# Pooled attention and a top-1 mixture of experts: gate stores, a query load and routing work moved to other places in the schedule

## The chip, the cores and the metric

The kernel runs on one core of a Trainium2 chip. The metric is the device time of one execution, in microseconds (us). A core has a matrix engine (TensorE, PE in the profile, with its weight loads as PEld), VectorE (DVE), ScalarE (ACT), GpSimd (POOL) and SyncE (SP), which issues most of the DMA transfers here. Each engine works off its own instructions in the order in which the program emits them, and engines wait for one another by semaphores. Schedules here are written by hand: moving a call in the source moves its instructions in the queues.

## The reference

```python
def _attn_ref(q, k, v):                      # 8 batches, 8 heads, 576 rows, 64 columns
    k_p = k.reshape(B, H, Sp, pool, D).mean(axis=3)      # pool = 8, Sp = 72
    v_p = v.reshape(B, H, Sp, pool, D).mean(axis=3)
    scores = scale * np.matmul(q, k_p.transpose(0, 1, 3, 2))
    attn = np.exp(scores - np.max(scores, axis=-1, keepdims=True))
    attn = attn / (np.sum(attn, axis=-1, keepdims=True) + 1e-09)
    return np.matmul(attn, v_p)

def _moe_ref(x, modality_id, w_gate, modality_bias, w1, w2):   # 4608 tokens, 512, 8 experts, 1024
    logits = x @ w_gate + modality_bias[modality_id]
    e_idx = np.argmax(logits, axis=1)
    probs = softmax(logits)
    gate_w = probs[np.arange(N), e_idx]
    for e in range(E):
        h = np.maximum(x[mask] @ w1[e], 0.0)
        out[mask] = gate_w[mask, None] * (h @ w2[e])
```

The attention's output, with the heads side by side in a row of 512, is the `x` of the second function. All is in 32-bit floats; the expert matmuls split each operand into a high and a low part and use three products.

## The kernel before, in words

**Attention.** Eight batches are worked off as 20 steps (`steps`, N = 20): of each pair of batches two steps of the first (two token tiles of 128 each), a mixed step with one tile of both batches' last 64 rows, and two steps of the second. Four pairs give four groups of nine tiles (`GROUPS`). The main loop (`for n in range(N + 1)`) emits in each step: the loads of that step (`loads(n)`), transposes of probabilities (`t_pe`, L692), scores (`s_pe`, L657 for a mixed tile, L663 for others), their maximum and difference on VectorE (`s_dve`, L670 and L673), exp on ScalarE (`s_act`), the weighted sum of values (`a_pe`, L727 and L731), its division on VectorE (`x_dve`, L750 to L760) and the query transposes of the next steps (`q_pe`, L638). The weighted sum has one PSUM buffer, the score tiles and the shared transpose tiles (tag `tr`) two each. Keys and values are summed over groups of eight rows, most of that on GpSimd (`fold`, L417 to L419), two batches ahead for keys and one for values.

**Hooks.** Work that belongs to no step is hung at places in the step: `hook_0` at its start, `hook_1` before the first weighted sum, `hook_q` after the query transposes, `hook_2` before the second weighted sum, `hook_3` at the end (of step N - 1 it is run early in step N).

**Loads.** `step_loads` lists which loads SyncE issues in which step, in that order; after them come the stores of token rows (`xs<-xb`, L767 and L770) that the step before made ready. `xs` is a table in DRAM with a row for each token: 512 values of the attention's output, then columns for the gate and for factors.

**Routing.** `route(g)` returns a list of small VectorE operations for a group: sums of the logits (L809), bias, maximum, difference and exp (`sub`, L816, L817), the choice of the expert (L820 to L822), the softmax's sum, `gates` (L844: the gate values; then four stores of 4-byte elements into the gate column of `xs`, L847 and L849), the running counts (L852), the rank matmuls `pe` (L829 to L833), ranks (L858 to L867) and nine rows `arow` (L869). They are put into `drip` and emitted one or two at a time at each `gap()`, between other VectorE work. `pe` is held: it is emitted only by `release()` in the step after one near whose end it stood first in the list. Groups 0 to 2 start two steps after their last step; the last group's list (`last_route`) is emitted after the loop and in the first expert slots. After group 1 the list also finds the first slots' tokens (`early_table`) and gathers them from `xs`.

**Start of the experts.** During the last attention steps the first expert's weights are loaded into `raw`, split into a high part on ScalarE (`split0`, L966) and a low part on VectorE (`split_lo`, L141), the first slot's tokens are transposed (`x_transposes`, L174 to L177), and the first layer of that slot is computed in eight blocks (`first0`, L184 on PE, L186 on ScalarE, L188 `h` on VectorE, by `finish()`), each with a PSUM tile of the tag `tr`. Then come the expert slots of 256 tokens (`part(s)`), in which PE runs two layers for each slot. Slot 0 has only the second layer left (`slot0`, L1365); `late` lists what small work is emitted after which of its eight blocks, such as `counts` (L1171), the rest of the last group's routing and the tables for later slots. For slot 1 the tokens are rearranged through DRAM (`blocks_out`, L246 for the copy of the gate column, L261, L266; `blocks_in`, L280).

Of the kernel before, what the change touches and what calls it, by code (L numbers as in the profile page):

```python
# [24 lines left out]
EARLY_GROUPS = 2  # L25
# [8 lines left out]
def kernel(  # L34
# [12 lines left out]
    nc = tc.nc  # L47
# [92 lines left out]
    def split_lo(f, eng):  # L140
        eng.tensor_sub(hl[f][:, 1, :], raw[f], hl[f][:, 0, :].bitcast(F32))  # L141
# [103 lines left out]
    def keep_gate(s, tt, eng):  # L245
        eng.tensor_copy(gc[:, 2 * s + tt:2 * s + tt + 1], xg[(2 * s + tt) % 4][:, D:D + 1])  # L246
# [4 lines left out]
    def blocks_out(s, tt):  # L251

        x = xg[(2 * s + tt) % 4] if tt < 2 else xe
        to = xg[(2 * s + 2 + tt % 2) % 4][:, 0:D]
        xp = to.rearrange("p (j k r) -> p j k r", j=NQ, r=QUAD)
        f = x[:, RX:RX + H].rearrange("p (k a o q) -> p k a o q", a=2, o=1, q=1)
        for a in range(2):
            xo = xp[:, 2 * a:2 * a + 2].rearrange("p j k r -> p k j r")
            xi = x[:, 0:D].rearrange("p (k a j r) -> p a k j r", k=ND, a=2, j=2)[:, a]
            if s < EARLY_SLOTS:  # L260
                nc.scalar.copy(xo, xi)  # L261
            else:
                nc.vector.tensor_tensor(xo, xi, f[:, :, a].to_broadcast([P, ND, 2, QUAD]), op=ALU.mult)
        if tt < 2:
            keep_gate(s, tt, nc.vector)
        nc.sync.dma_start(scr[s % 2, tt * P:(tt + 1) * P, :], to)  # L266

    def blocks_in(s, tt):
# [29 lines left out]
    with ExitStack() as actx:  # L298
# [302 lines left out]
        for g, (t0, n) in enumerate(GROUPS):  # L601
            for t in range(t0, t0 + n):
                tile_group[t] = (g, t - t0)
        drip, held, stores = [], set(), []

        def gap(n=2):

            for _ in range(n):
                if drip and drip[0] not in held:
                    drip.pop(0)()  # L610
# [180 lines left out]
        def route(g):  # L791
# [50 lines left out]

            def gates():
                V.reciprocal(gate[:, sl], sm)  # L844
                for z in range(2):
                    b = 2 * g + z
                    nc.sync.dma_start(xs[b * S:b * S + 512, D:D + 1].rearrange("(p j) o -> p (j o)", j=4),  # L847
                                      gate[:, t0 + 5 * z:t0 + 5 * z + 4], allow_slow_non_contiguous=True)
                    nc.sync.dma_start(xs[b * S + 512:(b + 1) * S, D:D + 1],  # L849
                                      gate[64 * z:64 * z + 64, t0 + 4:t0 + 5], allow_slow_non_contiguous=True)  # L850
            add(gates)
            add(lambda: V.tensor_add(cum[:, g + 1, :], cum[:, g, :], dc))  # L852
            held.add(pe)
# [91 lines left out]
        def at(hook, n, *fns):  # L945
            hook.setdefault(n, []).extend(fns)
# [19 lines left out]
            nc.scalar.copy(hl[f][:, 0, z * D:(z + 1) * D], raw[f][:, z * D:(z + 1) * D])  # L966

        for g in range(len(GROUPS) - 1):
            n = s1_of[2 * g + 1] + 2
            def start(g=g):  # L970
                ops = route(g)
                drip.extend(ops)
                if g == 0:
                    drip.extend(first_expert())
            at(hook_0, n, start)
            if g == EARLY_GROUPS - 1:
                at(hook_0, n, lambda: drip.extend(early_table()))
        for f, n in enumerate((10, 11, 11, 12, 13, 13, 14, 15)):
            at(hook_1, n, lambda f=f: (new_raw(f), load_w(0, f)))
        for f, n in enumerate((12, 13, 14, 15, 15, 16, 17, 19)):  # L980
            at(hook_1, n, lambda f=f: split0(f, 0))
            at(hook_2, n, lambda f=f: split0(f, 1))
        for f, n in enumerate((15, 15, 16, 16, 17, 17, 18, 19)):
            at(hook_3, n, lambda f=f: split_lo(f, nc.vector))
        at(hook_2, N - 3, lambda: x_transposes(0, xg, (0,)))
        at(hook_3, N - 3, lambda: x_transposes(0, xg, (1,)))
        at(hook_1, N - 2, lambda: keep_gate(0, 0, nc.gpsimd), lambda: keep_gate(0, 1, nc.gpsimd),
           lambda: blocks_out(1, 0), lambda: blocks_out(1, 1))
        at(hook_1, N - 1, lambda: blocks_in(1, 0), lambda: blocks_in(1, 1))
        for f in range(NF):  # L990
            at((hook_1, hook_2, hook_3)[(f + 1) % 3], N - 2 + (f + 1) // 3, lambda f=f: first0(f))

        at(hook_0, 5, modality_terms)

# [8 lines left out]


        step_loads = {}
        for n, fn, b in ((0, load_k, 2), (0, load_k4, 2), (0, load_v, 2), (0, load_v4, 2), (0, load_k, 3), (1, load_q, 2),
                         (1, load_v, 3), (1, load_k4, 3), (1, load_routing, None), (1, load_k, 4), (2, load_qmix, 1),
                         (2, load_v4, 3), (2, load_v, 4), (3, load_k4, 4), (4, load_q, 3), (4, load_k, 5), (4, load_v4, 4),
                         (4, load_v, 5), (5, load_k4, 5), (5, load_k, 6), (6, load_q, 4), (6, load_v4, 5), (6, load_v, 6),
                         (7, load_qmix, 2), (7, load_k4, 6), (7, load_k, 7), (9, load_q, 5), (9, load_v4, 6), (9, load_v, 7),  # L1010
                         (10, load_k4, 7), (11, load_q, 6), (11, load_v4, 7), (12, load_qmix, 3), (14, load_q, 7)):
            step_loads.setdefault(n, []).append((fn, b))

        def loads(n):
            for fn, b in step_loads.get(n, ()):
                fn(b) if b is not None else fn()
            while stores:
                stores.pop(0)()

        pool_k(0, (0,))  # L1020
        k_operand(0, 0)
# [25 lines left out]
        for n in range(N + 1):  # L1047
# [43 lines left out]
            run(hook_q, n)  # L1091
            if old:
                x_dve(old[0])
            gap(2)
            if nxt and n:
                q_act(n + 1, 1)
# [168 lines left out]
    for i, r in enumerate(EXTRA):  # L1265
# [14 lines left out]
    late = {  # L1280
        (0, 0): [lr[9], lr[7], lr[11], lr[8]],
        (0, 1): [lr[10]],
        (0, 3): [counts, lr[12]] + [fn for pair in zip(bases, lr[13:20]) for fn in pair] + [lr[20]],
        (0, 4): lr[21:24],
        (0, 5): lr[24:27],
        (0, 6): lr[27:],
        (1, 2): experts,
        (1, 3): columns,
        (1, 4): changes,
# [375 lines left out]
```

## Time and profile before

| what | us |
|---|---|
| median of 3 runs | 590.39 |
| the runs | 586.99, 590.39, 590.56 |
| the profiled execution | 587.84 |
| its span on the core | 586.0 |

Busy time in the span, from the page: PE 565.6 us (97%), PEld 494.6 (84%), DVE 371.3 (63%), ACT 277.6 (47%), POOL 183.5 (31%). By stages: the attention runs from the start to about 180 us, the expert slots from there to the end; the last slot's tail begins near 560.

How to read the rows below. A row of the busy time by stretch has the stretch, its length, then for PE, PEld, DVE, ACT and POOL the busy time with the number of instructions in brackets, then the granted TensorE clock as a share of full speed, the mean busy share of the 16 DMA engines and GB/s. A row in order of time has start, duration, engine, line, operation, what it writes and reads by name, partitions and elements, how many instructions were merged, and in brackets the engine's idle time before it with what ended it. Rows of SPq are issues of DMA transfers by SyncE; their duration is that of issuing, not of the transfer. The chain of waits gives start, duration and what the end of the execution hung on in that time. Matmuls are pipelined and their ends are modelled, so start-to-start distances are safer than durations.

### The profile page before, as it was taken

The numbers are of one execution on the slowest core, as the hardware profiler recorded it, in microseconds if no ns is written. First come the engines' busy times: TensorE is split into PE (matmuls) and PEld (weight loads), VectorE is DVE, ScalarE is ACT, GpSimd is POOL, SyncE is SP. The second block draws the span as 40 slices with busy tenths as digits, with TensorE's granted clock in tenths as the row PEclk, the third lists the DMA queues.
The fourth block names the chain that finished last, engine by engine and source line by source line (L and its number), as shares of the span: only waits on it lengthen the run. The fifth ranks groups of instructions, "written<-read, shape, count | busy, mean of one in ns | idle before, by whom it ended". The sixth has DMA issues, their size and how long they took to land.

```text
span 586.0 us, 11992 instructions
## 1 busy us (share of the span) xinstructions
PE 565.6 (97%) x3487; PEld 494.6 (84%) x3487; DVE 371.3 (63%) x939; ACT 277.6 (47%) x656; POOL 183.5 (31%) x290
## 2 busy tenths in 40 slices
PE   5999999999999999999999999999999999999995
PEld 5789888998898888888888888888888888888994
DVE  6887898778967676466456457856455497465211
ACT  2767676798652434333334336634334474334110
POOL 7679969854002202202202202212202203202102
PEclk9999999999999999999999999999999999999999
DMA  9999969995422423223223377233225743241101
GB/s 257 307 327 283 363 208 302 325 307 196 132 82 75 144 92 99 88 87 111 92 91 108 94 233 249 76 109 111 89 94 170 237 162 106 79 140 56 38 1 56
DMA packets 80926, 90.46 MB, mean 154 GB/s; under 512 B 17935, under 2 KB 56335, under 8 KB 80848
## 3 DMA queue, kind: packets, MB, share of 16 engines
q1 hardware_dynamic: 74928, 70.14, 38.4%
q0 software_dynamic: 5920, 19.44, 10.2%
q8 instruction: 29, 0.48, 0.3%
q14 instruction: 49, 0.40, 0.2%
HBM read 115.72 MB, written 28.62 MB: 246 GB/s over the span
## 4 chain that ended last, share of the span: by engine, by line
PE 80%; DMA 9%; DVE 7%; issue 1%; SPq 1%; ACT 1%; POOLq 0%; DVEq 0%; ACTq 0%
PE op L1365 32%; PE hp L210 20%; PE hp L214 10%; DMA q<-in_q_dram 5%; PE av L727 4%; PE hp L184 3%; PE sc L663 3%; DMA v<-in_v_dram 2%; PE av L731 2%; PE pp L692 1%; PE ph L184 1%; PE pq L638 1%; DMA k<-in_k_dram 1%; DMA out_dram<-obw,slw 1%; DVE hl L141 1%
## 5 line engine op out<-in xcount | busy, mean ns | idle before, releaser
L210 PE MATMUL hp<-xhl,hl 128*128 128x512 f32 x512 | 128.2, 392 | 0.0
L1341 POOL DMA_INDIRECT out_dram<-ob,sidx x34 | 36.2, 1065 | 278.6 <-DVE ob L1335 209.0
L218 DVE TENSOR_TENSOR ht<-ht,hp 128x256 f32<-128x256 f32 x128 | 53.1, 420 | 105.0 <-ACT ht L217 99.0
L210 PEld LDWEIGHTS hp<-xhl,hl 128*128 128x128 f32 x512 | 95.9, 187 | 21.3
L217 ACT COPY ht<-hp 128x256 f32<-128x256 f32 x128 | 47.3, 373 | 134.5 <-PE hp L214 111.4
L1365 PE MATMUL op<-hl,hx 128*128 128x512 f32 x429 | 104.2, 391 | 0.0
L1365 PEld LDWEIGHTS op<-hl,hx 128*128 128x128 f32 x429 | 78.3, 188 | 14.6
L1365 PE MATMUL op<-hl,hh 128*128 128x512 f32 x256 | 79.4, 391 | 0.0
L214 PEld LDWEIGHTS hp<-xhl,hl 128*128 128x128 f32 x512 | 69.1, 189 | 5.5
L214 PE MATMUL hp<-xhl,hl 128*128 128x256 f32 x512 | 70.3, 280 | 0.0
L1365 PEld LDWEIGHTS op<-hl,hh 128*128 128x128 f32 x256 | 45.8, 188 | 7.9
L727 PE MATMUL av<-vw,pt 128*128 128x146 f32 (+1 forms) x320 | 49.0, 292 | 1.3 <-DVE xb L760 1.2
L1365 PE MATMUL op<-hl,hlo 128*128 128x512 f32 x128 | 49.9, 390 | 0.0
L144 POOL DMA_INDIRECT xg<-xs,gidx x36 | 37.5, 1042 | 17.4 <-issue 9.8
L727 PEld LDWEIGHTS av<-vw,pt 128*128 128x128 f32 (+1 forms) x320 | 39.6, 180 | 3.1 <-DVE xb L760 0.9
L223 DVE SCALAR_TENSOR_TENSOR hlo<-ht,hh 128x256 fp32r<-128x256 f32 x64 | 27.0, 424 | 17.4 <-DVEq L1370 13.9
L663 PE MATMUL sc<-kt,qt 128*128 128x144 f32 x256 | 37.0, 288 | 0.8 <-DVE rs L858 0.4
L223 DVE SCALAR_TENSOR_TENSOR hx<-ht,hx 128x256 fp32r<-128x256 f32 x64 | 27.2, 426 | 15.7 <-DVEq L1370 14.3
L663 PEld LDWEIGHTS sc<-kt,qt 128*128 128x128 f32 x256 | 33.2, 190 | 1.6 <-DVE rs L858 0.7
L670 DVE TENSOR_REDUCE mx<-sc 128x8 f32<-128x576 f32 (+1 forms) x40 | 27.7, 692 | 6.6 <-PE sc L663 6.0
L731 PE MATMUL av<-vw,pt 128*128 128x146 f32 (+1 forms) x160 | 30.2, 291 | 0.1
L221 ACT ACTIVATE hx<-ht 128x256 fp32r<-128x256 f32 x64 | 26.4, 419 | 6.0 <-DVE ht L218 4.0
(271 smaller groups left out, 897.1 us busy)
## 6 DMA issues: line engine op xcount, KB each, us to landing
raw<-in_moe_w_dram SPq DMA_DIRECT2D x256, 256.0 KB
scr<-xg SPq DMA_DIRECT2D x35, 256.0 KB
xs<-xb SPq DMA_DIRECT2D x16, 528.0 KB
k<-in_k_dram SPq DMA_DIRECT2D x7, 1024.0 KB
v<-in_v_dram SPq DMA_DIRECT2D x7, 1024.0 KB
q<-in_q_dram SPq DMA_DIRECT2D x7, 1024.0 KB
y<-scr SPq DMA_DIRECT2D x108, 64.0 KB
v<-in_v_dram SPq DMA_DIRECT2D x16, 128.0 KB
```

The lines of the kernel that those rows point to most:

```text
L144: nc.gpsimd.indirect_dma_start(out=x, out_offset=None, in_=xs[0:rows, :], in_offset=IndirectOffsetOnAxis(idx[:, col:col + 1].bitcast(U32), 0),
L210: nc.tensor.matmul(hp[g % 2], hl[g][:, 0, d * P:(d + 1) * P], ab[:, d, :, 0:SLOT], start=(d == 0), stop=False)
L214: nc.tensor.matmul(hp[g % 2][:, 0:SLOT], hl[g][:, 1, d * P:(d + 1) * P], ab[:, d, 0, 0:SLOT], start=False, stop=(d == ND - 1))
L217: nc.scalar.copy(hts[g % 2], hp[g % 2][:, SLOT:2 * SLOT])
L218: nc.vector.tensor_add(hts[g % 2], hts[g % 2], hp[g % 2][:, 0:SLOT])
L223: nc.vector.scalar_tensor_tensor(hlo, hts[g % 2], 0.0, hh.bitcast(F32), op0=ALU.max, op1=ALU.subtract)
L663: nc.tensor.matmul(dst, qt[:, i, :], kt[b % NB][:, :, h * SPL:(h + 1) * SPL], start=True, stop=True)
L670: nc.vector.reduce_max(mx, scv, axis=AX.X)
L727: nc.tensor.matmul(av[hs, u, 2 * VC * gg:2 * VC * (gg + 1)], pt[:, c, hs], vw[y][:, c].rearrange("p a x -> p (a x)"), start=(gg == 0), sto ...
L731: nc.tensor.matmul(dst4[hs], pt4[:, hs], v4[y][:, 2 * u:2 * u + 2, :], start=False, stop=True)
L1341: nc.gpsimd.indirect_dma_start(out=out[:, :], out_offset=IndirectOffsetOnAxis(idx.bitcast(U32), 0), in_=ob, in_offset=None, bounds_check=N ...
L1365: nc.tensor.matmul(ot, l[:, ts_], hl[f][:, w, D:2 * D], start=(f == 0 and n == 0), stop=(f == NF - 1 and n == 2))
```

## The change

It does seven things. The gate stores of groups 0 to 2 are no longer emitted where the gates are computed but kept in `gate_stores` and emitted at the end of `loads` two steps later. The third batch's query load goes from behind the load of the fourth batch's keys to ahead of it; that key load moves from step 0 to step 1. The third group's routing (g = 2) starts at step 18 and not 16. Of the eight low parts of the first expert's weights five are emitted one or two steps later, two of these in `hook_1`. The first block of the first expert layer goes from `hook_2` to `hook_q` of step 18, with a `finish()` behind the division that follows it. The copies of slot 1's gate column go from VectorE to GpSimd. In slot 0 the counts and the rest of the last group's routing are emitted one block later each.

```diff
@@ blocks_out
         if tt < 2:
-            keep_gate(s, tt, nc.vector)
+            keep_gate(s, tt, nc.vector if s > 1 else nc.gpsimd)
@@
-        drip, held, stores = [], set(), []
+        drip, held, stores, gate_stores, now = [], set(), [], [], [0]
@@ route(g)
             def gates():
                 V.reciprocal(gate[:, sl], sm)
-                for z in range(2):
-                    b = 2 * g + z
-                    nc.sync.dma_start(xs[b * S:b * S + 512, D:D + 1].rearrange("(p j) o -> p (j o)", j=4),
-                                      gate[:, t0 + 5 * z:t0 + 5 * z + 4], allow_slow_non_contiguous=True)
-                    nc.sync.dma_start(xs[b * S + 512:(b + 1) * S, D:D + 1],
-                                      gate[64 * z:64 * z + 64, t0 + 4:t0 + 5], allow_slow_non_contiguous=True)
+
+                def put():
+                    for z in range(2):
+                        b = 2 * g + z
+                        nc.sync.dma_start(xs[b * S:b * S + 512, D:D + 1].rearrange("(p j) o -> p (j o)", j=4),
+                                          gate[:, t0 + 5 * z:t0 + 5 * z + 4], allow_slow_non_contiguous=True)
+                        nc.sync.dma_start(xs[b * S + 512:(b + 1) * S, D:D + 1],
+                                          gate[64 * z:64 * z + 64, t0 + 4:t0 + 5], allow_slow_non_contiguous=True)
+                if g < len(GROUPS) - 1:
+                    gate_stores.append((now[0] + 2, put))
+                else:
+                    put()
@@
         for g in range(len(GROUPS) - 1):
-            n = s1_of[2 * g + 1] + 2
+            n = s1_of[2 * g + 1] + (2 if g < EARLY_GROUPS else 4)
@@
-        for f, n in enumerate((15, 15, 16, 16, 17, 17, 18, 19)):
-            at(hook_3, n, lambda f=f: split_lo(f, nc.vector))
+        for f, n in enumerate((15, 15, 16, 17, 18, 19, 19, 20)):
+            at(hook_1 if f in (5, 7) else hook_3, n, lambda f=f: split_lo(f, nc.vector))
@@
         for f in range(NF):
-            at((hook_1, hook_2, hook_3)[(f + 1) % 3], N - 2 + (f + 1) // 3, lambda f=f: first0(f))
+            at((hook_1, hook_2, hook_3)[(f + 1) % 3] if f else hook_q, N - 2 + (f + 1) // 3, lambda f=f: first0(f))
@@ step_loads
-        for n, fn, b in ((0, load_k, 2), (0, load_k4, 2), (0, load_v, 2), (0, load_v4, 2), (0, load_k, 3), (1, load_q, 2),
+        for n, fn, b in ((0, load_k, 2), (0, load_k4, 2), (0, load_v, 2), (0, load_v4, 2), (1, load_q, 2), (1, load_k, 3),
@@ loads(n)
             while stores:
                 stores.pop(0)()
+            now[0] = n
+            while gate_stores and (gate_stores[0][0] <= n or n > N):
+                gate_stores.pop(0)[1]()
@@ main loop, after x_dve(old[0])
+            if n == N - 2:
+                finish()
@@ late
-        (0, 3): [counts, lr[12]] + [fn for pair in zip(bases, lr[13:20]) for fn in pair] + [lr[20]],
-        (0, 4): lr[21:24],
-        (0, 5): lr[24:27],
-        (0, 6): lr[27:],
+        (0, 4): [counts, lr[12]] + [fn for pair in zip(bases, lr[13:20]) for fn in pair] + [lr[20]],
+        (0, 5): lr[21:24],
+        (0, 6): lr[24:27],
+        (0, 7): lr[27:],
```

## The prediction

> **What bounds the kernel now.** I read the page first, then the busy time by stretch, then the waits and starts of the bound engine, then the queues behind those waits.
>
> ```profile
> span 586.0 us, 11992 instructions
> ```
>
> ```profile
> 20.00:80.00 60.00, 57.76 (x503) 53.23 (x501) 49.86 (x131) 41.04 (x111) 51.12 (x86) 1.00 1.03 330
> 80.00:140.00 60.00, 58.02 (x502) 53.77 (x501) 49.67 (x149) 49.00 (x127) 38.79 (x65) 1.00 0.85 270
> 140.00:160.00 20.00, 18.14 (x164) 16.31 (x163) 18.29 (x59) 13.39 (x37) 4.76 (x7) 1.00 0.44 135
> 160.00:180.00 20.00, 19.33 (x161) 18.96 (x161) 12.72 (x39) 9.50 (x24) 0.00 (x0) 1.00 0.25 79
> 180.00:186.00 6.00, 5.78 (x35) 4.53 (x34) 5.41 (x17) 1.40 (x3) 1.13 (x4) 1.00 0.14 56
> 186.00:560.00 374.00, 374.00 (x1926) 318.97 (x1925) 218.65 (x524) 152.20 (x334) 70.95 (x68) 1.00 0.37 117
> ```
>
> TensorE is the bound. Attention ends near 180 us; from 186 to 560 us PE is busy for 374.00 of 374.00 at a granted clock of 1.00, so nothing can be won there. The edits act between 20 and 186 us, where PE's idle time is 2.24 + 1.98 + 1.86 + 0.67 + 0.22 = 7.0 us. That is nearly the ceiling of any gain: 1.2% of the span. Here are two pieces of the chain of waits, and the PE rows that the edits can touch (start, time, idle time before the row and what ended it):
>
> ```profile
> 28.08 14.70 DMA q<-in_q_dram
> ...
> 43.98 0.98 PE sc L663 x8
> ```
>
> ```profile
> 40.76 1.15 PE L663 MATMUL sc<-kt,qt 128*128 128x144 f32 x8
> 42.92 0.63 PE L638 MATMUL pq<-ident,q 128*128 128x128 f32 x4 [1.01 <-DMA q<-in_q_dram]
> ...
> 62.98 0.71 PE L657 MATMUL sc<-kt,qt 128*64 128x144 f32 x8
> 63.67 0.63 PE L638 MATMUL pq<-ident,q 128*128 128x128 f32 x4
> ...
> 68.77 0.74 PE L727 MATMUL av<-vw,pt 128*128 128x146 f32 x4 [0.53 <-DVE xb L760]
> ...
> 100.41 0.71 PE L657 MATMUL sc<-kt,qt 128*64 128x144 f32 x8
> 102.43 0.63 PE L638 MATMUL pq<-ident,q 128*128 128x128 f32 x4 [1.31 <-DMA q<-in_q_dram]
> ...
> 103.48 0.74 PE L727 MATMUL av<-vw,pt 128*128 128x146 f32 x4
> ...
> 143.94 0.71 PE L657 MATMUL sc<-kt,qt 128*64 128x144 f32 x8 [0.63 <-ACT vg L527]
> 144.58 0.33 PE L704 MATMUL sc<-ident,pe 128*128 128x128 f32 x1
> ...
> 150.26 0.77 PE L727 MATMUL av<-vw,pt 128*128 128x146 f32 x4 [0.72 <-DVE xb L760]
> 157.13 1.25 PE L663 MATMUL sc<-kt,qt 128*128 128x144 f32 x8 [0.42 <-DVE rs L858]
> 161.79 0.66 PE L692 MATMUL pp<-ident,pe 128*128 128x128 f32 x4 [0.67 <-DVE h L188]
> ...
> 163.29 1.62 PE L184 MATMUL ph<-xhl,hl 128*128 128x256 f32 x12
> ...
> 185.01 0.17 PE L1171 MATMUL pcnt<-cum,ones 128*128 128x8 bf16 x1 [0.22 <-DVE cum L852]
> ```
>
> Eight of the rows name a wait, together 1.01 + 0.53 + 1.31 + 0.63 + 0.72 + 0.42 + 0.67 + 0.22 = 5.5 us. Ends of matmuls are modelled, so I price a wait from start to start: the eight score matmuls before 42.92 fill 0.98 (the chain's row), so PE could have gone on at 41.74 and lost 1.18, 0.17 more than the idle time shows. I add these 0.17 to the other waits.
>
> **Part A: third batch's queries ahead of keys.** SyncE's own rows:
>
> ```profile
> 27.40 0.58 SPq L316 DMA_DIRECT2D k<-in_k_dram  x1
> 28.08 1.27 SPq L349 DMA_DIRECT2D q<-in_q_dram  x1
> ...
> 63.56 0.37 SPq L316 DMA_DIRECT2D k<-in_k_dram  x1
> ```
>
> and what its queue waited for between 60 and 90 us (total, times, longest):
>
> ```profile
> SPq L847 <- DMA xs<-xb: 7.2, 1, 7.2
> ...
> SPq L316 <- DMA q<-in_q_dram: 1.2, 1, 1.2
> ```
>
> The two loads are neighbours in the queue, 1 MB each, and the queries land 14.70 us after their issue, behind the backlog. With the keys behind them they have 1 MB less in front: at 330 GB/s (20:80 row) 3.2 us, so they land near 39.6, ahead of 41.74. The 1.18 us go. What is late next: the fourth batch's queries are first read at 63.67. SyncE's key load of 63.56 had stood until they landed (its wait list has 1.2 us for this line on that transfer), so they land near 63.5, and the scores before took 0.69 from start to start, against 0.64 from 143.94 to the next row: PE came there just as they landed. The bytes ahead of them are the same in either order and DMA is full (share 1.03), so they land when they did and PE waits there for what it had won. What remains is VectorE's head start: its chain to 68.77 begins at scores that come 1.18 sooner, and the 0.53 + 0.17 = 0.7 that PE lost there can go. I take 0.7, with ends 0 and 1.2.
>
> The Trainium skill, DMA: Bandwidth & Descriptors, section Queues, rings and completion order, says that on each DMA engine descriptors are consumed in ring order. By that rule the fourth queries keep their time and A is 0.7; if landings could move with PE instead, A would be 1.2. The 14.70 us of the third queries, issued right behind the keys, agree with the rule.
>
> The keys land some 3 us later, near 42.8. POOL starts to fold them at 43.63 and has no gap before that: cover of 0.8 us. If it is gone, POOL's folds slip by the excess, and the next to be late are the fourth batch's pooled keys and values, which PE transposes.
>
> ```profile
> 43.63 1.28 POOL L417 TENSOR_TENSOR k<-k 128x512 f32<-128x512 f32 x1
> ```
>
> **Part B: gate stores two steps later.**
>
> ```profile
> 75.10 2.01 SPq L849 DMA_DIRECT2D xs<-gate  x1
> 84.37 0.54 SPq L847 DMA_DIRECT2D xs<-gate  x1
> ...
> 89.51 0.66 SPq L349 DMA_DIRECT2D q<-in_q_dram  x1
> ```
>
> ```profile
> 80.00:86.00 6.00, 5.68 (x44) 5.00 (x44) 6.00 (x17) 5.24 (x14) 3.76 (x8) 1.00 0.32 83
> ```
>
> The second gate pair of group 0 overwrites a column of token rows whose store has not landed, and SyncE stands still for 7.2 us; DMA falls to 83 GB/s. Behind it wait mixed queries, keys, two token stores and the sixth batch's queries (89.51), for which PE waits at 102.43. After the change these four kinds go out from 74 to 79 and use the empty 80:86; the gate stores then still wait for the same landing (about 84), and the queries follow at about 84.4 and some 1.4 for issuing the last pair, 85.8, with 1 MB at 330 GB/s (3.2 us) and little ahead of it: landing near 92. PE wants them at 100.41 + 0.64 = 101.05, so 1.38 us go. Next late: the second weighted sum of that step needs its PSUM buffer, which VectorE frees at 102.35 while it works off group 1's routing.
>
> ```profile
> 101.61 0.74 DVE L760 TENSOR_TENSOR xb<-av,r 128x256 f32<-128x256 f32 x2
> ```
>
> So that matmul starts near 102.4 and not at 103.48: I take 1.05, ends 0 (queries as late as before) and 1.4. Groups 1 and 2: SyncE waits little there, and their stores move past mixed queries, weight loads and token stores that have slack; the early gathers, near 140 us, read group 1's gates some 20 us after their new place. Nothing, unless the gathers catch them up; then POOL waits, with nothing queued for PE behind but one gate operand.
>
> **Part C: routing of the third group, low parts, first expert block, counts.** VectorE rows of steps 16 to 18:
>
> ```profile
> 140.92 1.20 DVE L809 TENSOR_REDUCE lgr<-lg 128x72 f32<-128x576 f32 x1
> ...
> 145.76 2.35 DVE L141 TENSOR_TENSOR hl<-raw,hl 128x1024 fp32r<-128x1024 f32 x2
> ...
> 156.19 0.75 DVE L670 TENSOR_REDUCE mx<-sc 128x8 f32<-128x576 f32 x1
> ...
> 160.33 0.41 DVE L869 TENSOR_SCALAR arow<-iota_b,rkf 128x128 bf16<-128x128 bf16 x2
> ...
> 163.11 0.42 DVE L188 SCALAR_TENSOR_TENSOR h<-ph,h 128x256 fp32r<-128x256 f32 x1
> ```
>
> VectorE is full from 140 to 160 (18.29 of 20), and PE's losses there are its lateness. They are the four from 143.94 (there ScalarE holds an exp of the routing) to 161.79: 0.63 + 0.72 + 0.42 + 0.67 + 4 x 0.17 = 3.1 us. Steps 16 and 17 lose the routing's first half (1.20 and eleven small ones at about 0.2, 3.3 us) and two low parts (2.35). The copies of the gates go to POOL, idle from 160 to 180 (0.00 busy), where nothing is queued behind them. I count these losses as gone up to step 18, and the first expert block, set ahead of the scores, covers the score buffer's wait: PE arrives 3.1 us earlier at 163.29. But that block's PSUM buffer is freed by the h of 163.11, done at 163.5. VectorE's stretch from 156.19 to there is 7.3 us (163.53 - 156.19); in it eight rank operations and four rows (twelve at about 0.2, by the rows of 0.41 for two: 2.3) give way to the routing's first half (3.3), whose small ones follow each other's results: I take 8.7 for the stretch. It stood behind two low parts, of which one is left (1.2 less), behind two gate copies (0.2) and behind PE's first two losses (0.63 + 0.72 + 2 x 0.17 = 1.7): it can start at 156.19 - 3.1 = 153.1. So h ends at 161.8, not 163.5, and the gain is held to 1.7 there.
>
> In step 20 the rank matmuls (0.3, they were in step 18) and the ranks between the divisions of the last weighted sums (four small ones, 0.3 on PE's way) cost 0.6; two late low parts fit into VectorE's idle time there (12.72 busy of 20). Five rows are left for after the loop, 0.8 us on VectorE ahead of the last group's routing. The counts, one block later, cover that and the 0.22 + 0.17 = 0.4 lost at 185.01. Sum: 1.7 - 0.6 + 0.4 = 1.5, of which I take 1.25, since PE can also be held by ScalarE, whose exp of the routing stands in step 18 behind the block's relu. Ends: 3.5 (all 3.1 and the counts) and -2 (VectorE enters step 18 as late as before: h comes 8.7 - 7.3 = 1.4 late, and 0.6).
>
> **Sum.** 0.7 + 1.05 + 1.25 = 3.0 us. The profiled execution took 587.84 us, its span 586.0 and 1.84 around it; it becomes 584.8. The runs shown are 586.99, 590.39 and 590.56, so the profiled one is 2.55 below the median. The mean of all four is 588.9, and from it I forecast 586.0.
>
> **The rivals.**
> First, all waits go, A 1.2, B 1.4, C 3.5: 6.1 less, 582.8. For it: each wait has its own cause that an edit names. Against it: VectorE's work is moved, not removed.
> Second, only one part works, as queries come when they did (B 0) or both query gains are given back at later buffers: 0.5 to 1.5 less, 588. For it: the gate stores still stand ahead of the sixth queries. Against it: 9 us of slack there.
> Third, slower: VectorE is late in steps 18 to 20. If it cannot start that stretch before 154.6 (163.5 - 8.7 - 0.6 + 0.4), C turns to loss, and at 156.19 it is -2.0; with the keys late for POOL and A at 0, B alone stands against it: some 1 us slower, 590. VectorE's idle time after 160 speaks against it.
>
> **How the numbers follow.** The forecast (gain 2 to 4.5) has 0.55, the first rival 0.15, the second 0.2, the third 0.1. One per cent, 5.9 us, is about what a measurement of this kernel can tell from no change. Nearly all of the first rival's 6.1 is needed to reach it, and spread of the runs (0.6% among those shown) adds a little: faster 0.16, slower 0.05, within it 0.79. The range runs from the first rival, 582.8, to the second at the upper runs, 590.5 - 1 = 589.5.
>
> **What would show it.** A: no wait on queries near 42, a first read of the fourth queries still near 63.6. B: SyncE without a 7 us wait near 80, DMA busy from 80 to 86, PE without idle time near 101. C: rows 143 to 157 without idle time, a new wait of PE on h before 163, counts without one. Wrong would be fourth queries that land earlier, or VectorE idle in step 18.

## The result and the profile after

The changed kernel takes 584.16 us (median of 22 runs, 582.39 to 586.09), the kernel before 587.50 us (22 runs, 585.62 to 592.68): a ratio of 0.9937, with a 95% interval of 0.992 to 0.9954. A second set, of 12 runs against 35, gave 0.9964 (0.9944 to 0.9985). Between them lies a gain of about 0.5%, 2.9 us (the mean of 0.63% and 0.36%, times 587). The kernel before against itself gave 0.9997 (0.998 to 1.0015). So the forecast of 3.0 us less and "within 1%" came true, and 584.16 lies in the range, 1.8 us under the 586.0 that was forecast. How the 3.0 us split did not come true.

First the page's first line of the changed kernel:

```profile
span 582.5 us, 11994 instructions
```

The busy time by stretch (columns as before; the last row is a stretch asked for by itself):

```profile
20.00:80.00 60.00, 57.28 (x496) 52.57 (x496) 50.39 (x127) 40.04 (x109) 52.09 (x88) 1.00 1.04 333
80.00:140.00 60.00, 59.27 (x508) 54.51 (x507) 49.50 (x154) 49.57 (x128) 37.55 (x63) 1.00 0.86 265
140.00:160.00 20.00, 19.68 (x172) 18.17 (x173) 16.96 (x48) 14.42 (x40) 5.71 (x9) 1.00 0.48 152
160.00:180.00 20.00, 19.33 (x159) 18.54 (x158) 15.19 (x48) 8.29 (x21) 0.00 (x0) 1.00 0.25 79
180.00:186.00 6.00, 6.00 (x37) 4.74 (x36) 5.41 (x20) 1.40 (x3) 2.00 (x4) 1.00 0.01 3
...
80.00:86.00 6.00, 5.78 (x44) 4.96 (x43) 5.75 (x22) 5.36 (x14) 2.40 (x6) 1.00 1.09 292
```

PE's idle time from 20 to 186 us falls from 7.0 to 2.72 + 0.73 + 0.32 + 0.67 = 4.4 us, but the first stretch has become worse (2.24 to 2.72), although the wait that A aimed at lies in it. The next view is PE's rows in order of time, with the idle time before a row in brackets.

```profile
40.42 1.15 PE L663 MATMUL sc<-kt,qt 128*128 128x144 f32 x8
41.41 0.60 PE L638 MATMUL pq<-ident,q 128*128 128x128 f32 x4
...
44.36 0.41 PE L508 MATMUL pv<-ident,vp 128*128 128x128 f32 x2 [0.27 <-POOL k L418]
...
62.77 0.66 PE L638 MATMUL pq<-ident,q 128*128 128x128 f32 x4
...
66.81 0.71 PE L657 MATMUL sc<-kt,qt 128*64 128x144 f32 x8 [0.52 <-ACT vg L527]
68.05 0.33 PE L704 MATMUL sc<-ident,pe 128*128 128x128 f32 x1 [0.53 <-DVE sb L673]
...
69.44 0.74 PE L727 MATMUL av<-vw,pt 128*128 128x146 f32 x4 [0.62 <-DVE xb L760]
...
101.59 0.66 PE L638 MATMUL pq<-ident,q 128*128 128x128 f32 x4
...
148.13 0.66 PE L727 MATMUL av<-vw,pt 128*128 128x146 f32 x4
...
158.61 0.60 PE L692 MATMUL pp<-ident,pe 128*128 128x128 f32 x4
...
163.00 0.60 PE L692 MATMUL pp<-ident,pe 128*128 128x128 f32 x4
164.28 1.65 PE L184 MATMUL ph<-xhl,hl 128*128 128x256 f32 x12 [0.67 <-ACT pt L697]
...
184.13 0.18 PE L1182 MATMUL pcnt<-cum,ones 128*128 128x8 bf16 x1
```

The third queries (41.41) and the sixth (101.59) are read with no idle time in brackets, the losses from 143 to 162 us are gone, and the counts (184.13) come without a wait. New are a small wait at 44.36, two at 66.81 and 68.05 us ahead of one that was there before (69.44, before 68.77), and one on ScalarE's copy at 164.28. The waits at 66.81, 68.05 and 69.44 are called the three losses below.

SyncE's rows show that B did to the queue what it says: mixed queries, keys and token stores now go out ahead of the gate stores, and the stand of 7.2 us is gone.

```profile
72.72 2.47 SPq L354 DMA_DIRECT2D qm<-in_q_dram  x2
75.29 3.24 SPq L323 DMA_DIRECT2D k<-in_k_dram  x1
...
81.20 1.15 SPq L849 DMA_DIRECT2D xs<-gate  x1
...
87.19 0.53 SPq L349 DMA_DIRECT2D q<-in_q_dram  x1
```

The span fell by 3.5 us, but PE's starts in the expert slots came only 2.2 us sooner, from 189 to 572 us alike. The other 1.3 us belong to the very end of the two executions, behind the last matmuls. One output store there stood on the chain of waits for 3.32 us before,

```profile
576.95 3.32 DMA out_dram<-obw,slw
```

and for 2.78 us after:

```profile
574.75 2.78 DMA out_dram<-obw,slw
```

That is 0.54 of the 1.3 us. In all thirteen other profiles of this study the end comes 0.5 to 1.4 us closer behind PE's last matmul than in the first profile of before, also in the unchanged kernel's second one (0.8 us). So it isn't counted to the change.

### The profile page after: what moved, and what is told of

Its sections match the earlier page's. It is cut to its first block, busy times and chain, and to the rows that moved or that the text cites. A ratio compares the mean times of both kernels' runs of the same rounds, so it can differ in the third digit from the quotient of the medians.

```text
span 582.5 us, 11994 instructions
## 1 busy us (share of the span) xinstructions
PE 566.0 (97%) x3487; PEld 494.6 (85%) x3487; DVE 371.4 (64%) x937; ACT 277.1 (48%) x656; POOL 185.2 (32%) x292
## 4 chain that ended last, share of the span: by engine, by line
PE 88%; DVE 3%; DMA 2%; ACT 2%; POOL 2%; issue 1%; SPq 1%; POOLq 0%; ACTq 0%; DVEq 0%
PE op L1376 34%; PE hp L210 20%; PE hp L214 10%; PE av L727 5%; PE sc L663 4%; PE hp L184 3%; PE av L731 3%; PE pp L692 2%; PE pq L638 2%; PE ph L184 2%; DMA v<-in_v_dram 2%; DMA out_dram<-obw,slw 1%; PE sc L657 1%; PE sc L520 1%; PE pk L461 0%
## 5 line engine op out<-in xcount | busy, mean ns | idle before, releaser
L144 POOL DMA_INDIRECT xg<-xs,gidx x36 | 38.8, 1076 | 17.5 <-issue 10.1
L141 DVE TENSOR_TENSOR hl<-raw,hl 128x1024 fp32r<-128x1024 f32 x24 | 29.0, 1217 | 0.2 <-issue 0.2
```

The lines of the kernel that those rows point to most:

```text
L144: nc.gpsimd.indirect_dma_start(out=x, out_offset=None, in_=xs[0:rows, :], in_offset=IndirectOffsetOnAxis(idx[:, col:col + 1].bitcast(U32), 0),
```

## The experiments

Two theories stood against each other at first. Theory 2 is the prediction's split: A 0.7, B 1.05, C 1.25. Theory 1 reads the first profile of the change: what A wins is lost again on VectorE between 64 and 70 us, B makes up for that near 101 us, and C brings 2.1 us. Later expectations number their own theories.

In all runs one execution is profiled and PE's start of the same matmul is compared with the first profile of before. The table gives what PE won (minus) or lost (plus) in each stretch against that profile, in us: the difference of start at the stretch's end less that at its beginning. The stretches end at the matmuls that started there at 39.8, 49.1, 75.7, 110.8, 163.8 and 189.1 us. The last column is the measured ratio to the kernel before.

| kernel | 40 to 49 | 49 to 76 | 76 to 111 | 111 to 164 | 164 to 189 | ratio (95%) |
|---|---|---|---|---|---|---|
| before, again | -0.05 | +1.64 | -0.83 | 0.00 | +0.02 | 0.9997 (0.9980 to 1.0015) |
| changed | -0.51 | +1.51 | -0.81 | -3.10 | +1.00 | 0.9937 (0.9920 to 0.9954) |
| changed, again | -0.53 | -0.09 | -0.73 | -3.03 | +1.00 | 0.9964 (0.9944 to 0.9985) |
| only A | -0.52 | +1.58 | -0.80 | +0.01 | +0.01 | 1.0004 (0.9983 to 1.0025) |
| only B | -0.10 | -0.10 | -0.74 | +0.02 | +0.01 | 1.0014 (0.9993 to 1.0035) |
| A and B | -0.51 | +0.26 | -0.67 | +0.02 | +0.01 | 0.9988 (0.9968 to 1.0008) |
| only C | -0.47 | +1.59 | -0.85 | -3.10 | +1.08 | 0.9971 (0.9945 to 0.9996) |
| exp later | -0.51 | +1.20 | -0.81 | -2.93 | +1.00 | 0.9967 (0.9947 to 0.9986) |
| routing back | -0.53 | +1.13 | -0.72 | -2.10 | +0.60 | 0.9949 (0.9925 to 0.9972) |
| fewer folds | -0.51 | -0.32 | -0.75 | -3.12 | +1.00 | not measured |
| first block back | -0.52 | +0.55 | -0.73 | -1.90 | +0.05 | 0.9948 (0.9927 to 0.9968) |
| low parts back | -0.52 | +1.34 | -0.82 | -2.03 | +0.05 | 0.9950 (0.9932 to 0.9969) |
| block and exp | -0.52 | +0.73 | -0.73 | -3.11 | +2.07 | 0.9959 (0.9942 to 0.9976) |

### The parts by themselves

Only A, against before:

```diff
-        for n, fn, b in ((0, load_k, 2), (0, load_k4, 2), (0, load_v, 2), (0, load_v4, 2), (0, load_k, 3), (1, load_q, 2),
+        for n, fn, b in ((0, load_k, 2), (0, load_k4, 2), (0, load_v, 2), (0, load_v4, 2), (1, load_q, 2), (1, load_k, 3),
```

> The kernel before with the third batch's queries ahead of the fourth batch's keys and nothing else. Theory 1 (A is given back at once): PE reads the third queries about 1.2 us sooner than before (42.92), but the small routing operations on VectorE in steps 6 and 7 (L816, L840) then stand longer behind GpSimd's folds, PE loses over 1.5 us between 64 and 70 (0.7 before) and is no sooner, or up to 0.7 us later, at the weighted sum that started at 75.9. Theory 2 (the prediction): about 0.7 us sooner at that weighted sum. By both the wait for the sixth batch's queries (102.43 before) is still there and takes up what PE has won or lost, so the whole time is that of before within 0.7 us.

Measured: the wait of 1.2 us is gone, 0.52 us of it are left at 49 us, and all of it is lost by 76 us (+1.58). The whole time shows no gain. Unexpectedly the wait for the sixth queries is gone too, although nothing of B is in this kernel.

Only B, against before:

```diff
-                for z in range(2):
...
+                gate_stores.append((now[0] + 2, put))
...
+            while gate_stores and (gate_stores[0][0] <= n or n > N):
+                gate_stores.pop(0)[1]()
```

> The kernel before with the gate stores of groups 0 to 2 two steps later and nothing else. Theory 1: the sixth queries land ahead of PE, and since PE was not made late in step 6 it is 1.0 to 1.4 us sooner from 104 to 140 us, more than the 0.14 us that the whole change shows there. Theory 2 (the prediction): 1.05 us, added to A's 0.7. Rival: the sixth queries still land behind PE's arrival and it wins under 0.4 us. Whole time: 1 us less by theories 1 and 2, within 0.4 of before by the rival.

Measured: PE is 0.74 us better from 76 to 111 us, less than both theories had; the whole time shows no gain (the interval excludes one of 1 us).

A and B together:

> The kernel before with A (queries ahead of keys) and B (gate stores later), without the moves of the routing, the low parts, the first block and the counts. Theory 1: PE is as in the whole change: up to 0.7 us later than before from 70 to 97 us and 0.1 to 0.3 us sooner from 110 to 140 us; A costs what B brings, the whole time is 0.1 to 0.5 us less than before, so less gain than B alone. Theory 2 (the prediction's split): 1.75 us less than before, sooner by that from 110 us on.

Measured: 0.9 us won from 40 to 111 us, neither the 1.75 of the prediction nor the 0.1 to 0.3 of theory 1; the whole time is 0.7 us less, with an interval from 1.9 less to 0.5 more.

Only C (routing, low parts, first block, gate copies and counts as in the change, loads and gate stores as before):

> The kernel before with the third group's routing two steps later, the low parts, the first block, the gate copies and the counts moved, and neither A nor B. Theory 1: C brings what the whole change shows from 143 us to the first expert slot, 2.1 us of PE's starts; whole time 2.1 us less. Theory 2 (the prediction): 1.25 us less, with PE held at the first expert layer until VectorE's h is done near 161.8. Rival: part of the 2.1 us needs the gate stores of group 2 out of the way; then C alone shows under 1.5 us.

Measured: 3.10 us won by 164 us, 1.08 given back, 2.0 left; by the whole time 1.7 us (0.2 to 3.2). This profile again has no wait for the sixth queries, without B, and from 40 to 49 us it is 0.47 us better than the first profile of before, without A: its wait for the third queries is 0.56 us. So C works alone, but the stretches before 111 us behaved in a way that the edits didn't explain: the loss of 1.5 us between 49 and 76 us came in kernels with A and without it.

### The same kernels once more

No edit.

> The kernel before, unchanged, profiled once more. Theory 1 (the waits of PE on the third and sixth queries depend on how far the loads happen to be in that execution): the landing of the fourth queries (63.54 us in the first profile, 61.04 to 63.3 in four single-part kernels) moves by up to 2 us, and if it is before 62.5 us PE loses some 1.5 us more at 64 to 70 us than the 0.7 of the first profile, and the wait at 102.43 us is shorter or gone. From 110 to 180 us PE's waits are the same as in the first profile within 0.1 us each, and the whole time is the same. Theory 2 (a profile repeats to 0.3 us at each wait, so differences of single-part kernels are those of their edits): landing within 0.5 us of 63.54, waits at 42.92, 68.77 and 102.43 us as before.

> The changed kernel, unchanged, profiled once more. Theory 1: PE's starts against the first profile of before differ from the first profile of the change by up to 1.5 us between 64 and 140 us, and what is won from 141 to 189 us is 2.1 us again within 0.1. If the fourth queries land after 62.8 us, the losses at 66.81, 68.05 and 69.44 us are together under 1 us (2.3 in the first profile). Theory 2 (a profile repeats): the three losses come again with 2.3 us together. No wait over 0.4 us on queries near 42 or 101 us by either. Whole time 0.5 to 0.9 per cent under before.

The second profile of the unchanged kernel, PE's rows:

```profile
43.48 0.63 PE L638 MATMUL pq<-ident,q 128*128 128x128 f32 x4 [0.98 <-DMA q<-in_q_dram]
...
68.34 0.71 PE L657 MATMUL sc<-kt,qt 128*64 128x144 f32 x8 [0.51 <-ACT vg L527]
69.58 0.33 PE L704 MATMUL sc<-ident,pe 128*128 128x128 f32 x1 [0.53 <-DVE sb L673]
...
70.97 0.74 PE L727 MATMUL av<-vw,pt 128*128 128x146 f32 x4 [0.63 <-DVE xb L760]
...
103.13 0.66 PE L638 MATMUL pq<-ident,q 128*128 128x128 f32 x4
```

Theory 2 falls. The wait for the third queries is back at nearly its size (in only C it was 0.56), so A removes a wait that comes again. The three losses of the changed kernel are there in the kernel before as well, and the wait for the sixth queries is not: SyncE issued them as late as in the first profile, but PE came to them at 103.13 us, 2.1 us later than the 101.05 at which it wanted them in the first profile, and found them landed.

```profile
84.53 0.54 SPq L847 DMA_DIRECT2D xs<-gate  x1
...
89.59 0.60 SPq L349 DMA_DIRECT2D q<-in_q_dram  x1
```

The changed kernel's second profile has the reverse: no three losses, only the wait that the first profile of before had there.

```profile
67.77 0.71 PE L657 MATMUL sc<-kt,qt 128*64 128x144 f32 x8
68.41 0.33 PE L704 MATMUL sc<-ident,pe 128*128 128x128 f32 x1
...
69.64 0.74 PE L727 MATMUL av<-vw,pt 128*128 128x146 f32 x4 [0.47 <-DVE xb L760]
```

Theory 1 was right that the stretch varies, and wrong in its condition: the fourth queries landed at 64.3 us in the second profile of before, later than in the first, and the losses came all the same.

### What makes the 1.5 us

The rows of VectorE and of GpSimd in step 6 of the changed kernel's first profile tell it. VectorE:

```profile
63.95 0.64 DVE L816 TENSOR_TENSOR lgr<-lgr,m 128x72 f32<-128x72 f32 x1
...
65.19 0.23 DVE L821 TENSOR_REDUCE m<-lgr 128x9 f32<-128x72 f32 x1
65.46 0.75 DVE L822 TENSOR_TENSOR oh<-w,m 128x72 bf16<-128x72 f32 x1
...
66.75 0.89 DVE L840 TENSOR_SCALAR sm<-sm 128x9 f32<-128x9 f32 x1
```

GpSimd:

```profile
63.78 0.72 POOL L417 TENSOR_TENSOR k<-k 128x256 f32<-128x256 f32 x1
...
65.40 0.72 POOL L417 TENSOR_TENSOR k<-k 64x256 f32<-64x256 f32 x1
...
67.00 0.61 POOL L503 TENSOR_TENSOR vw<-vp,m 128x256 f32<-128x256 f32 x1
```

Each of VectorE's three long operations ends within 0.1 us of the end of a GpSimd operation: 64.59 against 64.50, 66.21 against 66.12, 67.64 against 67.61. In the changed kernel's second profile the same L816 began just as a fold ended and took 0.23 us, L840 0.33. The Trainium skill says in SBUF — State Buffer, section SBUF: two separate sides, that VectorE and GpSimd share one pair of ports as an exclusive lock, taken by a VectorE operation with two inputs in SBUF or in a two-port mode, and held for a whole instruction; these rows agree, with 0.64 instead of 0.22 us for L816, and the reduction L821, with one input, took 0.23 us beside a fold. L840 has one input from SBUF; that it ran in a two-port mode isn't shown here, only that it stood until the end of the GpSimd operation. Which case comes up goes with where the folds stand against VectorE's work: the fold that opens step 6 started 0.37 to 0.85 us before L809 in the six profiles with the long operations and from 0.12 us before to 1.2 us after it in the seven without, which are all thirteen profiles with the folds unchanged. The later runs were made on three chips, and both cases came on each. What moves the folds isn't shown. The loads are likely: GpSimd's last wait for a load ahead of step 6 ended between 30 and 46 us in every profile.

The test takes three of GpSimd's folds away there, so this kernel's scores are not the right ones, and only its profile is read here:

```diff
+                        elif b == 4 and c:
+                            pass
                         elif b > 2 or c < 2:
...
-                    if i == 1:
+                    if i == 1 and b != 4:
                         fold(t4, kp4)
```

> The changed kernel without three of the four folds of the fifth batch's keys on GpSimd in step 6 (its scores are then those of older sums). Theory 1 (small VectorE operations of the routing stand until the GpSimd operation beside them ends): L812, L816, L822 and L840 all take 0.15 to 0.30 us (0.43, 0.64, 0.75 and 0.89 in the first profile of the change; L822 took 0.66 even in the profiles without the three losses), and PE's losses at the scores, the transpose and the weighted sum of steps 6 to 7 fall from 2.3 to at most 0.7 us together. Rival (PE, coming sooner, runs into VectorE's own work): the durations are short but the losses stay above 1.5 us.

VectorE's same operations in this kernel (its lines are two further down):

```profile
64.33 0.22 DVE L818 TENSOR_TENSOR lgr<-lgr,m 128x72 f32<-128x72 f32 x1
...
65.41 0.23 DVE L824 TENSOR_TENSOR oh<-w,m 128x72 bf16<-128x72 f32 x1
...
66.18 0.17 DVE L842 TENSOR_SCALAR sm<-sm 128x9 f32<-128x9 f32 x1
```

L822 fell to 0.23 us from 0.66 to 0.78, its value in those thirteen. PE's row of the weighted sum has no brackets any more:

```profile
68.15 0.74 PE L729 MATMUL av<-vw,pt 128*128 128x146 f32 x4
```

The three losses are gone, and with them the idle time of 0.46 to 0.63 us before the weighted sum that every other profile has and that the prediction, at 0.7, had put down to the late third queries. PE won 0.32 us from 49 to 76 us even against the first profile of before, which lacks the other two losses. By this one profile the rival falls.

### The third group's part

Here each of three edits of C is undone by itself in the changed kernel; the gate copies and the counts were not. By the whole time (ratios 0.9948 to 0.9950) none of the three kernels can be told from the changed one, so these readings rest on one profile each. The routing back at step 16:

```diff
-            n = s1_of[2 * g + 1] + (2 if g < EARLY_GROUPS else 4)
+            n = s1_of[2 * g + 1] + 2
```

> The changed kernel with the third group's routing back at step 16 (all else as changed). Theory 1 (the prediction's reason: VectorE is full in steps 16 to 18, and the routing's first half and two low parts are what make it late): the waits at 143.94 (0.63) and 150.26 us come back at least in part, PE's gain by 162 us falls from 3.1 us to between 1 and 2.2; the gain that is left at the first expert slot falls by 0.5 to 1.5 us. Rival (low parts and the first block alone do it): the gain at 162 us stays above 2.7 us and the whole time is that of the changed kernel.

```profile
145.39 0.71 PE L657 MATMUL sc<-kt,qt 128*64 128x144 f32 x8 [0.66 <-ACT vg L527]
```

The wait of PE on the gate operand, which ScalarE copies behind the routing's exp, is back; that at 150 us isn't. The gain by 164 us is 2.1 instead of 3.1, at 189 us 1.5 instead of 2.05: theory 1.

The first block back behind the scores:

```diff
-            at((hook_1, hook_2, hook_3)[(f + 1) % 3] if f else hook_q, N - 2 + (f + 1) // 3, lambda f=f: first0(f))
+            at((hook_1, hook_2, hook_3)[(f + 1) % 3], N - 2 + (f + 1) // 3, lambda f=f: first0(f))
...
-            if n == N - 2:
-                finish()
```

> The changed kernel with the first block of the first expert layer back in its old place, behind the scores, without the extra finish. Theory 1 (the block covers the wait of the scores for VectorE, and it shifts which PSUM buffer the later blocks get): the wait on ScalarE's pt at 164.28 us (0.84) goes, and a wait of 0.3 to 0.9 us on VectorE between 155 and 163 us comes; at 189 us PE's gain from 141 us on is 1.6 to 2.2 us. Rival (the block is what matters): that gain falls to under 1.2 us.

```profile
159.44 0.66 PE L692 MATMUL pp<-ident,pe 128*128 128x128 f32 x4 [1.11 <-DVE h L188]
```

The wait of 164.28 us goes, and one of 1.1 us on VectorE's h comes 5 us earlier (0.3 to 0.9 was expected). At 189 us 1.85 us are left, 0.2 less than in the change: theory 1, but for the size of the new wait.

The low parts back:

```diff
-        for f, n in enumerate((15, 15, 16, 17, 18, 19, 19, 20)):
-            at(hook_1 if f in (5, 7) else hook_3, n, lambda f=f: split_lo(f, nc.vector))
+        for f, n in enumerate((15, 15, 16, 16, 17, 17, 18, 19)):
+            at(hook_3, n, lambda f=f: split_lo(f, nc.vector))
```

> The changed kernel with the low parts of the weights back at their old steps. Theory 1 (two low parts out of steps 16 and 17, 2.4 us of VectorE's work, are a part of what makes VectorE punctual): waits of PE on VectorE of together 0.5 to 2 us come in steps 16 to 18, and the gain from 141 to 189 us falls from 2.05 to between 0.5 and 1.6 us. Rival (the routing alone matters): the gain stays above 1.8 us.

```profile
159.64 1.68 PE L184 MATMUL ph<-xhl,hl 128*128 128x256 f32 x12 [1.14 <-ACT qt L644]
```

One wait of 1.1 us near 160 us takes the place of that at 164.28, and 1.97 us are left: the rival, not theory 1. So the three edits don't add up. Undone one at a time they cost 0.1 to 0.55 us, while all of C brings 2.05, and the 0.1 of the low parts is hardly more than the two profiles of the change differ by (0.07). Between 159 and 167 us PE loses 0.9 to 1.3 us from start to start in each variant, and only the place changes.

### Two attempts at more

The exp of the routing two VectorE operations later, so that ScalarE doesn't stand before it:

```diff
-                nc.scalar.activation(ex, lg, AF.Exp)
...
-            add(lambda: V.reduce_max(m2, lg, axis=AX.X))
+            add(lambda: (V.reduce_max(m2, rs, axis=AX.X), nc.scalar.activation(ex, lg, AF.Exp)))
```

> The changed kernel, with the exp of the routing's logits (ScalarE, L817) emitted two VectorE operations later, and the masked logits written into another tile so that VectorE doesn't wait for that exp. Theory 1 (in step 6 ScalarE stands 1 to 2 us at that exp, which waits for a small VectorE operation that stands behind a fold of GpSimd; the copy of the gate operand, L527, is queued behind it and PE waits 0.7 us for it): the wait on vg goes, PE wins 0.3 to 1.2 us between 64 and 70 us in an execution in which the three losses occur, 0.2 to 0.5 in one in which they don't; whole time 0.3 to 1 us less than the changed kernel. Rival (VectorE itself is what is late, ScalarE only waits with it): the losses at the scores and the weighted sum (68.05, 69.44) take over what is won, whole time as the changed kernel within 0.2 us.

```profile
64.40 0.26 ACT L820 ACTIVATE ex<-lgr 128x72 f32<-128x72 f32 x1 [1.90 <-DVE lgr L816]
```

This missed its aim: the exp is still ahead of the query copies in ScalarE's queue and ScalarE stands idle for 1.9 us before it. It says nothing on the theory; the time is that of the changed kernel.

The second goes further, with the exp right before the sum that reads it, and the fourth block right behind the third:

```diff
-                nc.scalar.activation(ex, lg, AF.Exp)
...
-            add(lambda: V.reduce_sum(sm, ex, axis=AX.X))
+            add(lambda: (nc.scalar.activation(ex, lg, AF.Exp), V.reduce_sum(sm, ex, axis=AX.X)))
...
-            at((hook_1, hook_2, hook_3)[(f + 1) % 3] if f else hook_q, N - 2 + (f + 1) // 3, lambda f=f: first0(f))
+            at((hook_1, hook_2, hook_3)[(f + 1) % 3] if f not in (0, 3) else (hook_q, hook_1)[f // 3], N - 2 + (f + 1) // 3, lambda f=f: first0(f))
```

> The changed kernel with two further moves: the fourth block of the first expert layer right behind the third (it stood behind the transposes whose PSUM buffer it needs), and the exp of the routing emitted right before the sum that reads it, so that it no longer stands ahead of the query copies in ScalarE's queue. Theory 1: the wait of 0.84 us on ScalarE's pt near 164.28 us goes and the gain of PE from 141 to 189 us is 2.6 to 2.9 us (2.05 in the change); ScalarE no longer stands over 1 us before the exp in step 6, and PE's wait on vg there (0.69) falls under 0.3. Whole time 0.6 to 1.5 us under the changed kernel, ratio to before 0.992 to 0.995. Rival (the next wait takes it over: the transposes then wait for VectorE's h of the third block): the gain stays within 0.3 us of 2.05 and the whole time is that of the changed kernel.

```profile
66.94 0.71 PE L657 MATMUL sc<-kt,qt 128*64 128x144 f32 x8
...
165.74 0.74 PE L727 MATMUL av<-vw,pt 128*128 128x146 f32 x4 [1.07 <-DVE xb L760]
...
184.95 0.17 PE L1181 MATMUL pcnt<-cum,ones 128*128 128x8 bf16 x1 [0.60 <-DVE cum L857]
```

ScalarE no longer stands before the exp in step 6. The row at 66.94 has no wait on the gate operand, but L816 was short in this execution (0.22 us), and then that wait is absent without the edit too, as in the changed kernel's second profile; so it doesn't show that the edit removes it. The wait of 164.28 became one of 1.07 on VectorE at the next weighted sum, and VectorE, which now waits 1.18 us for the exp in the last group's routing, is late for the counts. Only 1.0 us of C's 2.05 is left. The rival that the next wait takes over was right, and worse than expected. Neither version is faster than the changed kernel.

## Why the prediction was right, and where its parts were not

**The total was right by luck: errors of opposite sign cancelled.** The terms were A 0.7, B 1.05 and C 1.25. What the profiles show is A 0.05 to 0.5, B 0.75 in some executions and nothing in others, and C 2.05. By whole times only C stands out, with 1.7 us of the 2.9; A and B gave no gain alone and 0.7 us together, with an interval that holds zero. How much of the remaining 1.2 us is theirs stays open.

**Part A.** The wait at 42 us went, as said, in all ten profiles with the new order. It stood in both profiles of before and in only C (0.7 to 1.2 us; in only B 1.1 us were lost at the same place, which the trace puts down to ScalarE). "PE waits there for what it had won", at the fourth queries, was wrong in place. Of the 1.18 us won, 0.42 were given back right away at the transposes of probabilities, for which the waits name ScalarE, and 0.43 at 44.36, where PE came ahead of the pooled values that VectorE and GpSimd make. With A 0.51 to 0.53 us are won by 49 us, against 0 to 0.10 in both profiles of before and in only B, but 0.47 in only C. So A is worth 0.4 to 0.5 us in most executions and almost nothing in one like only C's, inside the 0 to 1.2. The step that failed is "the 0.53 + 0.17 = 0.7 that PE lost there can go", before the weighted sum of 68.77: that wait was not the late scores' but GpSimd's, since it stayed at 0.47 + 0.17 = 0.6 in the changed kernel's second profile and went when the folds were left out. Whether the fourth queries keep their landing can't be read off: SyncE's key load behind them started at 60.3 to 65.8 us in the fourteen profiles, with no order by A. The cover of 0.8 us on GpSimd's side held in seven of the ten profiles with A; in three GpSimd waited 0.2 to 0.85 us for the later keys.

**Part B.** There is no stand of 7 us any more, and DMA is busy for 1.09 from 80 to 86 us, as described. The sixth queries went out later than the 85.8 us that were put, at 87.19 us in the first profile of the change and in only B at 90.40, behind the 89.51 of before. They still landed sooner, with the keys ahead of them in the queue out some ten us earlier (75.29 us, 87.19 before): by the transfers' semaphores near 102 us in both profiles of before, and between 93 and 100 in the ten with B. The size, 1.05, took it for granted that PE arrives at 101 us as in that one profile. It arrives so only when it lost nothing in step 6. Then B is worth about 0.75 us against the one profile that has the wait (only B, -0.74; changed again, -0.73). In only B 0.31 of the 1.39 won at the queries goes to VectorE at the weighted sum that the prediction named, as put, and 0.35 more, which were not put, at those up to 107.5 us. When step 6 costs PE its 1.5 us, there is no wait to remove: the second profile of before shows this without B. And in only A and only C the loads ran some 2.3 us ahead, which did the same. The prediction's second rival ("only one part works") had this outcome for A and B, though not the cause.

**Part C.** That VectorE's lateness is the loss was right: routing back at step 16 brings a wait back. The four losses were put at 3.1 us, and PE won 3.0 to 3.1 by 164 us, in both profiles of the change and in only C. The step that failed is the hold to 1.7, "that block's PSUM buffer is freed by the h of 163.11, done at 163.5". In the first profile of before that block starts at 163.29 already, 0.2 us ahead of the end of that h, and behind the end of a copy of ScalarE's:

```profile
162.48 0.59 ACT L697 COPY pt<-pp 128x512 f32<-128x512 f32 x1 [0.94 <-PE pp L692]
```

In the changed kernel's first profile the same block starts 3.2 us sooner and without a wait, although the same h (163.11 before) comes only at 160.75. The block after it, at 164.28 (166.60 before), is the one that is held, until ScalarE has copied the transposes that stand right ahead of it:

```profile
160.06 1.62 PE L184 MATMUL ph<-xhl,hl 128*128 128x256 f32 x12
...
163.64 0.59 ACT L697 COPY pt<-pp 128x512 f32<-128x512 f32 x1 [1.55 <-PE pp L692]
```

PE's lead fell by 0.95 us there, where 3.1 - 1.7 = 1.4 was put; that a hold came at all where one was put is luck. That the block gets the PSUM buffer of those transposes fits this, and with the first block back in its old place, which shifts the order of the buffers, the wait is gone. The step for step 20, 0.6, measured 0.4 (PE's lead from 168 to 174 us), and the counts brought 0.35 where 0.4 was put. So 3.1 - 0.95 - 0.4 + 0.35 = 2.1, where 1.25 had been taken, and the extra 0.25 for ScalarE was not needed on top of the hold. VectorE wasn't idle in step 18, as said.

**The base.** The prediction called the profiled execution 2.55 us below the median and set its sum against the mean of four runs, 588.9. By the 22 runs the kernel before takes 587.50, so the profiled execution's 587.84 was the better base: 584.8 from it lies 0.7 us from the measured 584.16. Its waits were taken for the kernel's, and the largest of the eight (1.31) was in that execution alone of the four profiles with the old gate stores.

## What to carry to other kernels

Profile the unchanged kernel twice before pricing its waits: a wait that comes again within 0.1 us is worth an edit, up to what the next wait leaves of it, and one that depends on when loads land is worth the share of executions that have it. Where two engines take turns at being late, undoing single edits shows little while the group of edits brings much. A buffer's releaser should be checked against the rows: a block that starts before an operation ends wasn't waiting for it. A small operation on VectorE beside GpSimd's folds should be priced at up to a whole GpSimd operation, and at the rest of the one before it too (0.89 us here), above all where ScalarE's queue stands behind it.

## What the runs showed of the hardware

VectorE's operations with two inputs of 128 x 72 (L812, L816, L822) took 0.42 to 0.78 us where they came during a GpSimd addition, and a 128 x 9 operation with one input (L840) 0.33 or 0.89; with the folds left out they took 0.22 to 0.23 and 0.17 us. The long ones ended 0.03 to 0.09 us behind the end of the GpSimd operation. Reductions beside the same folds stayed at 0.21 to 0.23. Two profiled executions of the kernel before differed by 1.6 us in what PE lost from 49 to 76 us, and by 0.01 us from 111 to 189 us, where no load is waited for.
